# Masking softmax tiles on GpSimd: two affine selects per block in place of one multiplication by a stored mask

## The chip, the core and the metric

The kernel runs on one core of one Trainium2 chip. The metric is the device time of one execution in microseconds (us). Five engines work side by side, each through its own list of instructions in order, and wait for one another by semaphores: TensorE (PE, matrix products and transposes, with its weight loads PEld), VectorE (DVE), ScalarE (ACT), GpSimd (POOL) and SyncE (SP, which here only issues DMAs). POOL and ACT also issue DMAs. PE writes to PSUM; DVE and ACT read PSUM and SBUF; POOL works on SBUF alone.

## The reference

Eight batches, eight heads, 576 positions, head size 64. Causal attention over a window of 64 positions, then a multiplicative feed-forward network over all 4608 tokens.

```python
scores = scale * np.matmul(q, k.transpose(0, 1, 3, 2))
rel = pos[:, None] - pos[None, :]
mask = (rel >= 0) & (rel < 64)
scores = np.where(mask, scores, -1000000000.0)
attn = softmax(scores)
x = np.matmul(attn, v)          # -> (4608, 512)
a = x @ w1
b = x @ w2
out = ((a * b) @ w3) @ w_out
```

## The kernel before

The order of the work on each engine is written out by hand in the program. There are two strands that share PE.

**Attention.** A batch is cut into three segments of 192 queries (`SEGS`), and a segment into two head pairs, so a batch has six score tiles, d = 6b to 6b + 5, and the kernel 48. `scores(d)` computes K times Q transposed on PE (L303) into PSUM, takes the exponential with ACT into an fp16 tile `pt` in SBUF (L307), and then POOL sets to zero what lies outside the window, in place (L312). It does so by multiplying with a stored 0/1 mask of 128 x 256, broadcast over four head rows. In the first segment two instructions do it (4 x 128 and 4 x 64 columns), in the other two one instruction over 1024 columns. `pt` has six buffers. `values(d)` multiplies `pt` with V on PE (L339 in the first two batches, L355 later); V has columns of ones beside it, so the same product yields the row sums. ACT turns these into reciprocals (logarithm and exponential, L345/L346, L361 to L363), and DVE writes the normalised result to `xT` (L347, L364/L365).

**Preparation of a batch.** K and Q arrive in fp32 by SP's DMAs (`load_qk`, tile `stage`) and are cast to fp16 by POOL (L226, 1152 columns each, four per batch), or, in the first two batches, arrive as fp16 in `rows` by POOL's DMAs and are copied by DVE and ACT (also L226). PE transposes them (L262), DVE and ACT copy the result out of PSUM (L266). V comes by POOL's DMAs into `v16` (`load_v`, L241); two of its blocks overlap others by half, so `copy_v` copies halves of 64 partitions from SBUF to SBUF on DVE (L245, and L247 for one block). V of batch 0 takes another way: it is copied by DVE (L226, twice, "k<-rows" in the profile, since the tile is shared), transposed twice by PE and evicted.

**Feed-forward.** First w3 and w_out are folded into one matrix `wc_sb` (`fold_t` L493/L494, `fold_mm` L502/L504), between the score tiles of batch 0. Then groups of 512 tokens pass `ffn_ab` (L433 on PE, into the three `f_ps` banks of PSUM; ACT copies one product out, L438, DVE multiplies the other with it, L439) and `ffn_o` (L451 on PE, DVE copies out to `t2k`, L453, SP stores). In the steady part a tick of the attention is placed between these pieces by due times, and each tick carries one event of the next batch (`late`): a load, a cast, a transpose or a copy of V.

POOL's list therefore holds, in this order: constants, weight loads, the mask's making (`make_mask`, a memset and two affine selects on 128 x 256), and then masks, casts and DMA issues as the program writes them. At the start it reads: masks of tiles 0 and 1, two loads of w1/w2, masks of 2 and 3, two loads of K of batch 1, masks of 4 and 5, two loads of Q, two more of w1/w2, five of V of batch 1. DVE's two copies of V of batch 0 stand behind the masks' first tiles in time, and PE's transposes of V wait for both.

Of the kernel before, what the change touches and what calls it, by code (L numbers as in the profile page):

```python
# [9 lines left out]
FP16 = mybir.dt.float16  # L10
I32 = mybir.dt.int32
ALU = mybir.AluOpType
# [3 lines left out]
P = 128  # L16
# [128 lines left out]
def kernel(  # L145
# [11 lines left out]
    nc = tc.nc  # L157
# [23 lines left out]
    const = fast.enter_context(tc.tile_pool(name="const", bufs=1))  # L181
# [87 lines left out]
    def keys_of_v(b, js, into, cps):  # L269
# [4 lines left out]
        for j, tp, cp in zip(js, into, cps):  # L274
            cp(v16s[b % 2][:, :, j].rearrange("p c (a e) -> p c a e", a=2)[:, :, :, 0:D],
               tp.rearrange("p c (a e) -> p c a e", a=2))

    probs, lns = {}, {}
    mask = const.tile([P, 2 * P], FP16)

    def make_mask():
        nc.gpsimd.memset(mask, 1.0)
        pat = [[-64, 2], [1, P]]
        nc.gpsimd.affine_select(out=mask, in_=mask, pattern=pat, compare_op=ALU.is_ge,
                                fill=0.0, base=64, channel_multiplier=-1)
        nc.gpsimd.affine_select(out=mask, in_=mask, pattern=[[-s, m] for s, m in pat], compare_op=ALU.is_ge,
                                fill=0.0, base=63 - 64, channel_multiplier=1)

    def scores(d):

        b, r = divmod(d, 6)
        si, jp = divmod(r, 2)
        kT, qT = turned["k", b], turned["q", b]
        seg = SEGS[si]
        w = sum(blk[2] for blk in seg)
        s_ps = ps_s.tile([P, 2, 2, 256], FP32, name="s_ps")
        for jj in range(2):
            j = 2 * jp + jj
            c0 = 0
            for (k0, q0, n, _) in seg:  # L300
                for a in range(2):
                    half = slice(a * D, a * D + D)
                    nc.tensor.matmul(s_ps[:, a, jj, c0:c0 + n], kT[half, j, k0:k0 + P], qT[half, j, q0:q0 + n],  # L303
                                     start=True, stop=True, skip_group_check=True)
                c0 += n
        pt = sb.tile([P, 2, 2, 256], FP16, name="pt", bufs=6)
        nc.scalar.activation(pt[:, :, :, 0:w], s_ps[:, :, :, 0:w], AF.Exp, bias=-SHIFT, scale=scale)  # L307

        rows = pt.rearrange("k a j n -> k (a j) n")
        for (lo, n, m0) in [(0, 128, 128), (128, 64, 0)] if si == 0 else [(0, 256, 0)]:  # L310
            sl = rows[:, :, lo:lo + n]
            nc.gpsimd.tensor_tensor(sl, sl, mask[:, m0:m0 + n].unsqueeze(1).to_broadcast([P, 4, n]), ALU.mult)  # L312
        probs[d] = pt

    def values(d, pool=None):
# [78 lines left out]
    def tick(u):  # L394

        b, r = divmod(u, 12)
        d = u // 2
        if u % 2 == 0 and d < ND:
            scores(d)
        ev = late.get(r, [])  # L400
        for e in ev:
            if e[0] == "t":
                event(b, *e)
        if u % 2 == 1 and 12 <= d - 1 < ND:
            values(d - 1)
        for e in ev:
            if e[0] != "t":
                event(b, *e)
        n, m = divmod(u - LAG - 4, 4)
        if m == 3 and n >= 6:  # L410
            keep_sums(n)
# [63 lines left out]
    def load_wo(half):  # L475
        cols = slice(half * 256, half * 256 + 256)
        nc.gpsimd.dma_start(out=wo16[:, :, cols], in_=moe_w_out[:, cols].rearrange("(e p) m -> p e m", p=P))
# [28 lines left out]
    rows = 2 * 3 * B  # L506
# [38 lines left out]
    for n in range(2, 4):  # L545
        load_w3(n)
    load_wo(1)
    make_mask()

    def bank(pool, name):  # L550

# [16 lines left out]
    transposes(0, "q", 0, 1, 2, into=three(), cps=[act_cp, dve_cp, act_cp])  # L568
    keep_busy(6)
    scores(0)  # L570
    keep_busy(4)
    fold_t(0)
    scores(1)
    fold_t(1)
    for i in range(2):
# [94 lines left out]
    for g in range(1, NG):  # L670
        part = [lambda g=g, fc=fc: ffn_ab(g, fc) for fc in range(8)] + \
               [lambda g=g, t=t: ffn_o(g, t) for t in range(4)]
        lo = need[g]
# [58 lines left out]
```

## Time and profile before

| what | us |
|---|---|
| three runs | 304.34, 304.97, 307.15 (median 304.97) |
| the profiled execution, its own time | 304.97 |
| its span, from first to last instruction | 303.1 |
| mean granted clock of PE | 0.977 |
| POOL busy, of it the masks (L312) | 174.3, 97.6 |
| POOL idle before masks, waiting for ACT | 89.4 |
| masks of 1024 columns, 32 of them, mean | 2.146 |
| masks of 512 columns, 16, mean | 1.152 |
| masks of 256 columns, 16, mean | 0.666 |
| casts by POOL, 1152 columns, 24, mean | 1.149 |
| copies of V by DVE, L245, 14: shortest, median, longest | 0.289, 0.874, 3.584 |

Busy time is the sum of what the profiler shows of an engine's instructions; issues of DMAs count as busy on POOL. A line of the groups gives line, engine, operation, output and inputs with partitions x columns and type, then the number of instructions, the busy time in us with the mean of one in ns, and the idle time before them with what ended it. A line of a timeline gives start, length, engine, line, operation and count, and in brackets the idle time before the first. Instructions that follow closely with the same line and tiles are merged into one. A table of windows gives, for each stretch, its length, then for PE, PEld, DVE, ACT and POOL the busy time and the number of instructions, and behind them the granted clock of PE, the DMA share and GB/s.

### The profile page before, as it was taken

How to read it: one execution, taken by the hardware profiler on the slowest of the kernel's cores; microseconds unless marked ns; L12 is line 12 of the kernel's file. 1: busy time of each engine (PE TensorE's matmuls, PEld its weight loads, DVE VectorE, ACT ScalarE, POOL GpSimd, SP SyncE). 2: the span in 40 equal slices, each digit the busy share in tenths (PEclk: the TensorE clock that was granted, in tenths of full speed). 3: DMA queues.
4: the chain of work that ended last, by engine and by line, in shares of the span. 5: the costliest groups of instructions: out<-in, count | busy, mean ns of one | idle time of the engine just before them, and what ended most of it. 6: DMA issues, size and time to landing. Idle time of an engine off the chain costs nothing.

```text
span 303.1 us, 6174 instructions
## 1 busy us (share of the span) xinstructions
PE 281.6 (93%) x2425; PEld 164.2 (54%) x2425; DVE 194.6 (64%) x277; ACT 170.2 (56%) x281; POOL 174.3 (58%) x153
## 2 busy tenths in 40 slices
PE   8793999969999999998999899997999999999993
PEld 8673977524554555554555588453555544454442
DVE  1468456443686766779868966679688665455441
ACT  2652447656357738775686455385748766742310
POOL 9899710299558856596669452792776543320400
PEclk9897799998999999999999999999999999999999
DMA  6999999658558928292829190780059003003013
GB/s 253 220 210 204 211 190 39 243 229 55 94 205 336 79 84 286 85 73 79 282 104 112 72 320 29 75 146 0 3 92 130 0 25 117 2 0 140 1 38 109
DMA packets 48449, 37.68 MB, mean 124 GB/s; under 512 B 34160, under 2 KB 38512, under 8 KB 48416
## 3 DMA queue, kind: packets, MB, share of 16 engines
q0 software_dynamic: 38960, 11.14, 37.0%
q1 hardware_dynamic: 9024, 24.79, 22.3%
q10 hardware_dynamic: 432, 1.31, 1.2%
q8 instruction: 20, 0.33, 0.4%
q14 instruction: 13, 0.11, 0.1%
HBM read 38.80 MB, written 9.44 MB: 159 GB/s over the span
## 4 chain that ended last, share of the span: by engine, by line
PE 74%; DVE 11%; issue 8%; ACT 5%; POOL 1%; DVEq 0%; POOLq 0%; ACTq 0%
PE f_ps L433 36%; PE f_ps L451 14%; PE tp L262 5%; PE s_ps L303 4%; PE o_ps L355 4%; PE f_ps L502 3%; PE tp L528 3%; DVE k L226 2%; DVE t2k L453 2%; DVE v L245 1%; PE f_ps L493 1%; DVE ab L439 1%; PE o_ps L339 1%; DVE v L247 1%; DVE xT L365 1%
## 5 line engine op out<-in xcount | busy, mean ns | idle before, releaser
L312 POOL TENSOR_TENSOR pt<-pt,mask 128x512 f16<-128x512 f16 (+1 forms) x64 | 97.0, 1527 | 89.4 <-ACT pt L307 89.3
L433 PE MATMUL f_ps<-xT,w_sb 128*128 128x512 f16 (+1 forms) x640 | 136.4, 361 | 4.4 <-DVE t2k L453 2.4
L433 PEld LDWEIGHTS <-w_sb 128*128 128x128 f16 x640 | 60.1, 98 | 56.5 <-issue 7.2
L451 PE MATMUL f_ps<-wc_sb,ab 128*128 128x512 f16 (+1 forms) x296 | 66.9, 373 | 0.1
L439 DVE TENSOR_TENSOR ab<-f_ps,a_sb 128x512 f16<-128x512 f32 x72 | 49.6, 691 | 25.3 <-PE f_ps L433 23.7
L307 ACT ACTIVATE pt<-s_ps 128x1024 f16<-128x1024 f32 (+1 forms) x48 | 45.7, 952 | 26.8 <-PE s_ps L303 23.6
L438 ACT COPY a_sb<-f_ps 128x512 f32<-128x512 f32 x72 | 41.7, 579 | 29.0 <-PE f_ps L433 28.4
L451 PEld LDWEIGHTS <-ab 128*128 128x128 f16 x296 | 27.6, 98 | 27.6 <-issue 0.3
L364 DVE TENSOR_TENSOR xT<-o_ps,r 64x384 f16<-64x384 f32 x36 | 19.7, 548 | 34.3 <-ACT r L363 34.2
L361 ACT ACTIVATE ln_s<-o_ps 64x384 f32<-64x384 f32 x36 | 17.5, 487 | 32.6 <-PE o_ps L355 32.6
L453 DVE COPY t2k<-f_ps 128x512 f32<-128x512 f32 (+1 forms) x36 | 24.4, 681 | 11.1 <-PE f_ps L451 10.7
L241 POOL DMA_DIRECT2D v<-in_v_dram x35 | 30.1, 868 | 2.3 <-DMA rows<-in_k_dram 1.1
L355 PEld LDWEIGHTS <-v 128*128 128x128 f16 x288 | 17.9, 98 | 9.0 <-issue 0.8
L355 PE MATMUL o_ps<-pt,v 128*128 128x128 f16 (+1 forms) x288 | 20.7, 215 | 0.4 <-DVE xT L365 0.4
L303 PEld LDWEIGHTS <-kT 64*128 64x128 f16 x384 | 10.7, 95 | 18.6 <-issue 17.3
L365 DVE TENSOR_TENSOR xT<-o_ps,r 64x384 f16<-64x384 f32 x36 | 20.2, 561 | 0.5
L363 ACT ACTIVATE r<-ln_s 128x384 f32<-128x384 f32 x36 | 18.8, 522 | 1.1
L245 DVE COPY v<-v 64x512 f16<-64x512 f16 x14 | 19.1, 1365 | 0.4
L303 PE MATMUL s_ps<-qT,kT 64*128 64x128 f16 (+1 forms) x384 | 18.5, 217 | 0.2
L266 DVE COPY kT<-tp 128x768 f16<-128x768 f16 x19 | 18.0, 950 | 0.0
L362 ACT ACTIVATE ln_s<-o_ps 64x384 f32<-64x384 f32 x36 | 17.4, 482 | 0.4
L226 POOL CAST k<-stage 128x1152 f16<-128x1152 f32 x12 | 13.7, 1149 | 3.5 <-issue 3.5
(88 smaller groups left out, 237.4 us busy)
## 6 DMA issues: line engine op xcount, KB each, us to landing
out_dram<-t2k SPq DMA_DIRECT2D x35, 256.0 KB
stage<-in_k_dram SPq DMA_DIRECT2D x13, 576.0 KB
stage<-in_q_dram SPq DMA_DIRECT2D x13, 576.0 KB
v<-in_v_dram POOLq DMA_DIRECT2D x28, 128.0 KB, 4.4
w_sb<-in_moe_w_dram POOLq DMA_DIRECT2D x4, 512.0 KB, 12.7
ab<-in_moe_w_dram POOLq DMA_DIRECT2D x2, 512.0 KB, 7.8
ab<-in_moe_w_out_dram POOLq DMA_DIRECT2D x2, 512.0 KB, 12.7
xT<-in_moe_w_dram POOLq DMA_DIRECT2D x2, 512.0 KB, 14.4
```

Of the source, the lines that this page charges most:

```text
L241: nc.gpsimd.dma_start(out=vh[lo:P, c], in_=v[b, :, s0:s0 + P - lo, :].rearrange("h s d -> s h d"))
L245: dve_cp(vh[0:D, c], vh[D:P, c - 1])
L303: nc.tensor.matmul(s_ps[:, a, jj, c0:c0 + n], kT[half, j, k0:k0 + P], qT[half, j, q0:q0 + n], start=True, stop=True, skip_group_check=True)
L307: nc.scalar.activation(pt[:, :, :, 0:w], s_ps[:, :, :, 0:w], AF.Exp, bias=-SHIFT, scale=scale)
L312: nc.gpsimd.tensor_tensor(sl, sl, mask[:, m0:m0 + n].unsqueeze(1).to_broadcast([P, 4, n]), ALU.mult)
L355: nc.tensor.matmul(o_ps[:, jj, o0:o0 + n], v16[:, si * 2 + bi, j0 + jj, a * D:a * D + P], pt[:, a, jj, c0:c0 + n], start=first, stop=(bi = ...
L365: nc.vector.tensor_tensor(xs[D:P], o_ps[D:P, :, 192:384], r[D:P], ALU.mult)
L433: nc.tensor.matmul(d[:, f * n + c0:f * n + c1], w[:, dc, (fc + f) * P:(fc + f + 1) * P], xT[:, dc, xc:xc + c1 - c0], start=first, stop=(dc ...
L438: act_cp(a_sb[:, 0:nf * n], a_ps[:, 0:nf * n])
L439: nc.vector.tensor_tensor(ab[:, fc:fc + nf, lo:hi], b_ps[:, 0:nf * n].rearrange("p (f n) -> p f n", f=nf), a_sb[:, 0:nf * n].rearrange("p ...
L451: nc.tensor.matmul(o_ps[:, 0:c1 - c0], ab[:, fc, t * P:t * P + P], wc_sb[:, fc, c0:c1], start=(fc == 0), stop=(fc == 7))
L453: cp(o_sb[:, c0:c1], o_ps[:, 0:c1 - c0])
```

## The change

`scores` no longer multiplies by the stored mask. It applies two affine selects in place to each block: the first keeps an element where the position in the window is not below zero, the second where it is below 64, and both write 0.0 elsewhere. The stored mask and its making are gone. The table `MASKS` lists for each segment the blocks: offset, number of 128-column blocks, columns, and the numbers of the condition. In the first segment there are two blocks (128 and 64 columns in each of the four head rows), hence four instructions per tile where there were two. In the other segments there is one block of 2 x 128 in each of four rows, 1024 columns, hence two instructions where there was one. The second select of a pair reads what the first wrote and waits for it by POOL's own semaphore; a multiplication waits for ACT alone. In all, 64 multiplications, a memset and two selects go, and 128 selects come. The lists of PE, DVE, ACT and SP are the same before and after, and so is the place of each mask in POOL's list. The words that came with the change speak of copies of V's halves of batch 1 and of loads and casts of K and Q of batch 2; the diff holds nothing of these.

```diff
     probs, lns = {}, {}
-    mask = const.tile([P, 2 * P], FP16)
-
-    def make_mask():
-        nc.gpsimd.memset(mask, 1.0)
-        pat = [[-64, 2], [1, P]]
-        nc.gpsimd.affine_select(out=mask, in_=mask, pattern=pat, compare_op=ALU.is_ge,
-                                fill=0.0, base=64, channel_multiplier=-1)
-        nc.gpsimd.affine_select(out=mask, in_=mask, pattern=[[-s, m] for s, m in pat], compare_op=ALU.is_ge,
-                                fill=0.0, base=63 - 64, channel_multiplier=1)
+    MASKS = [[(0, 1, 128, 0, 0), (128, 1, 64, 64, 0)]] + 2 * [[(0, 2, 128, 64, -64)]]
...
         rows = pt.rearrange("k a j n -> k (a j) n")
-        for (lo, n, m0) in [(0, 128, 128), (128, 64, 0)] if si == 0 else [(0, 256, 0)]:
-            sl = rows[:, :, lo:lo + n]
-            nc.gpsimd.tensor_tensor(sl, sl, mask[:, m0:m0 + n].unsqueeze(1).to_broadcast([P, 4, n]), ALU.mult)
+        for (lo, nb, n, off, step) in MASKS[si]:
+            sl = rows[:, :, lo:lo + nb * n]
+            pat = [[0, 4], [step, nb], [1, n]]
+            if nb == 1:
+                pat = [[0, 4], [1, n]]
+            nc.gpsimd.affine_select(out=sl, in_=sl, pattern=pat, compare_op=ALU.is_ge,
+                                    fill=0.0, base=off, channel_multiplier=-1)
+            nc.gpsimd.affine_select(out=sl, in_=sl, pattern=[[-s, m] for s, m in pat], compare_op=ALU.is_ge,
+                                    fill=0.0, base=63 - off, channel_multiplier=1)
         probs[d] = pt
...
     load_wo(1)
-    make_mask()
```

## The prediction, made before the run

> **What bounds the kernel.** I read the page first: busy times and the chain that ended last.
>
> ```profile
> PE 281.6 (93%) x2425; PEld 164.2 (54%) x2425; DVE 194.6 (64%) x277; ACT 170.2 (56%) x281; POOL 174.3 (58%) x153
> PE 74%; DVE 11%; issue 8%; ACT 5%; POOL 1%; DVEq 0%; POOLq 0%; ACTq 0%
> ```
>
> PE sets the end. POOL, the only engine whose instructions the change touches, has 1% of the chain and is idle for 42% of the span, so its own sum decides nothing. But DVE has 11%, so I went to the timeline of PE (start, us, engine, line, names, count, in brackets the idle time before and what ended it) for the places where it stood still.
>
> ```profile
> 28.21 0.82 PE L262 MATMUL o_ps<-ident,k 128*128 128x128 f16 x6 [4.60 <-DVE k L226]
> 67.22 0.43 PE L339 MATMUL o_ps<-pt,v 128*64 128x64 f16 x12 [2.73 <-DVE v L247]
> 143.43 1.02 PE L433 MATMUL f_ps<-xT,w_sb 128*128 128x512 f16 x4 [0.98 <-DVE t2k L453]
> 172.38 1.03 PE L433 MATMUL f_ps<-xT,w_sb 128*128 128x256 f16 x8 [0.95 <-DVE t2k L453]
> 173.84 1.91 PE L433 MATMUL f_ps<-xT,w_sb 128*128 128x256 f16 x16 [0.43 <-DVE t2k L453]
> 205.24 1.89 PE L433 MATMUL f_ps<-xT,w_sb 128*128 128x512 f16 x8 [0.39 <-DVE ab L439]
> 208.98 1.89 PE L433 MATMUL f_ps<-xT,w_sb 128*128 128x512 f16 x8 [1.40 <-DVE ab L439]
> ```
>
> These are 11.5 us, and each has a DVE instruction behind it. The timelines of DVE and then POOL tell why:
>
> ```profile
> 21.27 6.88 DVE L226 COPY k<-rows 128x1152 f16<-128x1152 f16 x2
> 49.59 0.45 DVE L226 COPY k<-rows 128x1152 f16<-128x1152 f16 x1
> 87.00 0.29 DVE L245 COPY v<-v 64x512 f16<-64x512 f16 x1
> 135.50 3.58 DVE L245 COPY v<-v 64x512 f16<-64x512 f16 x1
> ```
>
> ```profile
> 134.59 1.16 POOL L226 CAST k<-stage 128x1152 f16<-128x1152 f32 x1
> 135.70 2.13 POOL L312 TENSOR_TENSOR pt<-pt,mask 128x1024 f16<-128x1024 f16 x1
> 137.77 1.14 POOL L226 CAST k<-stage 128x1152 f16<-128x1152 f32 x1
> ```
>
> A copy of V takes 0.29 us at 87.00, when POOL is still, and 3.58 at 135.50, where it ends (139.08) 0.17 behind the last of three POOL instructions that follow one another without a pause (138.91). The two copies at 21.27 take 6.88 together, and 0.45 each at 49 to 51 us, where POOL is still. So a DVE copy between SBUF tiles stands while POOL computes. That is the path by which masks reach PE: how long POOL runs without a pause, not how much it does.
>
> **The change, part by part.** Orders on PE, DVE, ACT and SP stay the same; only POOL's list changes: 64 multiplications go, 128 selects come in pairs, and the building of the mask (L282 to L286) goes. The words given with the change (V's copies, loads of batch 2) are not what the diff does, so nothing is priced for them.
>
> The price of a select, from the groups by form (busy us, mean ns):
>
> ```profile
> L284 POOL TENSOR_SCALAR_AFFINE_SELECT mask<-mask 128x256 f16<-128x256 f16 x1 | 0.4, 401 | 0.1
> masks.py:199 POOL TENSOR_SCALAR_AFFINE_SELECT ident<-ident 128x128 f16<-128x128 f16 x1 | 0.3, 291 | 0.1
> L312 POOL TENSOR_TENSOR pt<-pt,mask 128x1024 f16<-128x1024 f16 x32 | 68.5, 2146 | 39.5 <-ACT pt L307 39.5
> ```
>
> 401 - 291 = 110 ns for 128 more columns: 0.86 ns a column and 0.18 us fixed, hence 1.06 us for 1024 columns, 0.62 for 512, 0.40 for 256. (One more row of the pattern also costs 110 this way, so eight rows of 128 give the same 1.06.) The CAST, one input too, has 1152 columns in 1.15. The other bound is proportion, 401 x 4 = 1.60; I take 1.06, as the CAST is nearest in size. The second select of a pair waits for the first: L284 starts at 13.00 and L286 at 13.48, so 0.08 of pause. A pair over 1024 is 2.20 against 2.15; a first-segment tile (512 and 256) is 2.20 against 1.82. POOL gets 32 x 0.05 + 16 x 0.38 = 7.7 us more, hidden under its 129 us of idle time. Behind a mask POOL also issues DMAs, up to 0.8 us later at the start, but early loads land one behind another (w_sb 12.7 us after issue), so the queue stays fed. The mask's building (1.2 us) ended in front of a wait of 1.27 for ACT: zero. The selects' waits queue only POOL's own next masks, casts and issues.
>
> The pause is what pays. A waiting DVE copy has its place between the two selects, 1.06 us into a mask. Whether 0.08 us is enough no row shows for sure. For it: the copies of 0.29 end 0.14 to 0.17 after POOL falls still, so they start at once; and the first copy of 21.27 (4.59 us, the longest of its line, so to 25.86) got through at 25.46, where POOL went from an issue to a mask with 0.01 between. Against it: at 135.75 and 137.83 one instruction followed another and the copy did not get in; but there the next POOL instruction waited for nothing of POOL's own.
>
> - Start. Masks begin at 15.14; two tiles 4.40, two issues 1.57: the third tile starts at 21.11, its first select ends at 22.17. The first copy (asked for at 21.27) runs there and ends at 22.5. The second I let wait through a select and the next tile's first select, to 24.62, and end at 24.95. PE goes on at 25.0 instead of 28.21: 3.2 less. Bounds: 0 (no pause used, or 0.5 lost) and 4.3 (it gets in at 23.6).
> - Clock. The granted clock fell behind that stop:
>
> ```profile
> 28.20:32.00 3.80, 3.79 (x36) 3.79 (x37) 1.65 (x2) 1.52 (x2) 3.80 (x5) 0.50 1.24 207
> 32.00:36.00 4.00, 4.00 (x48) 3.84 (x46) 2.70 (x5) 1.17 (x2) 2.95 (x4) 0.81 1.14 211
> ```
>
> The seventh figure is the clock: half until about 33.5. Without a stop of that length 5.3 us of work at half clock becomes 2.65 if PE alone counts; V's copies out of PSUM stand in it too, so I take 2.2 of the 2.65. Bound below: 0.
> - At 64.5. The two copies of V of batch 1 stand here one behind the other. Tiles 6 and 7 put POOL 0.4 to 0.5 later, so L245 meets the second CAST, runs between tile 8's selects (66.4), and L247 meets the second select and perhaps both casts of q, to 67.2 at best and 69.9 at worst: PE goes on 1.1 earlier to 2.7 later; the half clock from 67.6 to 71.0 (1.75 us on eight matmuls, 3.58 for 1.83) may go or double. I take +1.0.
> - Batches 3 to 6. 0.98 + 0.95 + 0.43 + 0.39 + 1.40 = 4.15 of stops. At 135.50 the copy would end at 136.9, 2.1 earlier, and the next one (now 140.86) would come before the mask at 140.06. I take 3.8 of 4.15; bounds 0 and 4.15.
>
> Sum: -3.2 - 2.2 + 1.0 - 3.8 = -8.2. Span 303.1 - 8.2 = 294.9; with the 1.9 outside the span (304.97 - 303.1; this execution is also the median) **296.8 us**.
>
> [...] The row: the copy of 135.50 waited through three POOL instructions, 3.3 us. [...]
>
> **Rivals.**
> - *The pause is too short.* Copies wait through both selects as through one multiplication, 0.05 to 0.4 longer. For: the two refusals above. Time: 304.97 + 0.5 at the start or at 64.5, about 305.5 (303 to 307.5).
> - *A dear select makes POOL the bound* (slower). Place: the steady batches. A batch now costs POOL 97.6/8 = 12.2 in masks, 4.5 in casts, 4.3 in V issues: 21 of the some 31 us between first tiles (145.71 to 177.01). It decides when masks take 22, that is from some 1.9 us per 1024-column select. At 2.15 (the multiplication's rate in each of a pair) masks take 4 x 4.4 + 2 x 3.8 = 25, POOL 34 a batch: 3 us over on five or six batches, less what the pauses bring: about 318 (308 to 325). Against: three rows of the trace at 0.86 ns; for: none has a pattern with a zero step or 1024 columns.
> - *The middle eats the start*: both copies at 64.5 wait through the casts with half clock twice, +2.7 + 1.75, with half of the other gains: about 304.
>
> **Chances.** Forecast 0.60 (its own range 292 to 300.5: all gains at their ends, or the start at half). Short pause 0.20, dear select 0.15, middle 0.05. Range 292 to 307: nearly all of the forecast and the first and third rival, some 0.8; what is left out is mostly the dear select. Faster by over 1% (below 301.9; 1% is about what a measurement here tells from no change) 0.61, within 0.22, slower (over 308.0) 0.17.
>
> **What will show it.** Selects of 128x1024 at about 1.06 us; L226's two DVE copies together under 4 us; PE's stop before L262 under 1.5 and no half clock behind it; copies of L245 never over 1.6; no stops at t2k and ab in batches 3 to 6; the stop before L339 near 64 us not shorter. Wrong if selects are over 1.6, or if copies still end only where a pair and its followers end.

## The result, and the profile after

The changed kernel took 292.05 us (median of 4 runs, 291.53 to 292.87) where the kernel before took 305.36 (4 runs, 304.34 to 307.15). The ratio is 0.9561, with a 95% interval of 0.9508 to 0.9613: 13.3 us less. Times here and below are medians of all runs, ratios those of the runs within 1.5% of the fastest of the same kernel. The forecast was 296.8, 8.2 us less, in a range of 292 to 307, at whose lower edge the result lies. The direction and the path were as predicted; the size was not. The profiled execution took 292.37 us, its span is 290.5 and the mean granted clock 0.991 (before 304.97, 303.1, 0.977).

The busy times and the chain that ended last, from the page of the changed kernel:

```profile
PE 276.5 (95%) x2425; PEld 160.4 (55%) x2425; DVE 179.4 (62%) x277; ACT 170.2 (59%) x281; POOL 179.3 (62%) x214
PE 81%; DMA 5%; DVE 4%; ACT 3%; POOL 3%; issue 1%; SPq 0%; POOLq 0%; DVEq 0%; ACTq 0%
```

POOL is 5 us busier, DVE 15.2 us less busy with the same 277 instructions, and DVE's part of the chain fell from 11% to 4%. POOL was given more work, and what fell is the time in which DVE's copies stand: its copies from SBUF to SBUF took 30.8 us together before and 15.3 after, the rest of DVE 168.9 in both.

The timeline of PE, at the places where it stood before:

```profile
23.22 0.51 PE L262 MATMUL o_ps<-ident,k 128*128 128x128 f16 x6 [0.40 <-DVE k L226]
59.70 0.45 PE L338 MATMUL o_ps<-pt,v 128*64 128x64 f16 x12 [2.15 <-DVE v L247]
133.74 1.89 PE L432 MATMUL f_ps<-xT,w_sb 128*128 128x512 f16 x8
161.44 3.66 PE L432 MATMUL f_ps<-xT,w_sb 128*128 128x256 f16 x32
194.04 1.89 PE L432 MATMUL f_ps<-xT,w_sb 128*128 128x512 f16 x8
196.21 1.89 PE L432 MATMUL f_ps<-xT,w_sb 128*128 128x512 f16 x8
```

The stop of 4.60 us before V's transposes (L262) is 0.40. The five stops of the batches, 0.98, 0.95, 0.43, 0.39 and 1.40, are gone: these lines have no brackets, and the groups of 4, 8 and 16 that the stops had cut apart are whole again (x8, x32). Of the stops shown before, only the one near 58 us is left, 2.15 for 2.73. The granted clock (seventh figure) of the two stretches around the first place:

```profile
23.00:28.00 5.00, 4.40 (x68) 4.14 (x69) 3.43 (x6) 3.00 (x5) 4.86 (x6) 1.00 1.29 202
28.00:33.00 5.00, 4.57 (x74) 3.74 (x70) 2.44 (x5) 2.91 (x7) 4.93 (x7) 1.00 1.24 210
```

The half clock that fell behind that stop is gone. Now the same two places on DVE and then POOL as in the prediction, the start and the copy of batch 3, on DVE:

```profile
20.48 2.68 DVE L226 COPY k<-rows 128x1152 f16<-128x1152 f16 x2
127.93 1.67 DVE L245 COPY v<-v 64x512 f16<-64x512 f16 x1
```

and on POOL:

```profile
21.64 1.20 POOL L310 TENSOR_SCALAR_AFFINE_SELECT pt<-pt 128x1024 f16<-128x1024 f16 x1
22.81 1.31 POOL L308 TENSOR_SCALAR_AFFINE_SELECT pt<-pt 128x1024 f16<-128x1024 f16 x1
...
127.23 1.16 POOL L226 CAST k<-stage 128x1152 f16<-128x1152 f32 x1
128.33 1.11 POOL L308 TENSOR_SCALAR_AFFINE_SELECT pt<-pt 128x1024 f16<-128x1024 f16 x1
129.52 1.09 POOL L310 TENSOR_SCALAR_AFFINE_SELECT pt<-pt 128x1024 f16<-128x1024 f16 x1
130.57 1.14 POOL L226 CAST k<-stage 128x1152 f16<-128x1152 f32 x1
```

The copy of 127.93 comes up during a cast (to 128.39). It does not get in there, where the select follows at once; it stands through the first select (to 129.44) and ends at 129.60, 0.16 behind it, so it got in at the gap before the second. Before, the like copy stood through a cast, a multiplication and a cast, 3.58 us. At the start the two copies take 2.68 together where they took 6.88, and the second ends at 23.16, so it got in where the second select of one tile ends (22.84) and the first of the next begins. That next select is shown 1.31 long where its kind takes 1.11, as if here POOL had stood for the copy.

To see where the time came from, the start of the same PE instruction is compared in both traces:

| PE instruction | before | after | ahead | gained since the row above | predicted |
|---|---|---|---|---|---|
| first product of the fold | 16.60 | 15.81 | 0.79 | 0.8 | 0 |
| first transpose of V, batch 0 | 28.21 | 23.22 | 4.99 | 4.2 | 3.2 |
| after the half clock | 33.52 | 26.58 | 6.94 | 1.95 | 2.2 |
| values that wait for V of batch 1 | 67.22 | 59.70 | 7.52 | 0.6 | -1.0 |
| before the first stop of the batches | 132.18 | 124.61 | 7.57 | 0.05 | 0 |
| after the last stop of the batches | 208.98 | 196.21 | 12.77 | 5.2 | 3.8 |
| end of the last product | 298.42 | 285.34 | 13.08 | 0.3 | 0 |

Behind the last product 0.5 us is given back (4.7 to 5.2 us to the end of the span), which leaves the 12.6 us between the two profiled executions.

The price of the selects, from the groups by form (busy us, mean ns):

```profile
L308 POOL TENSOR_SCALAR_AFFINE_SELECT pt<-pt 128x1024 f16<-128x1024 f16 x32 | 35.7, 1114 | 34.5 <-ACT pt L300 34.5
L310 POOL TENSOR_SCALAR_AFFINE_SELECT pt<-pt 128x1024 f16<-128x1024 f16 x32 | 35.2, 1099 | 2.3
```

The 2.3 us of idle time before 32 second selects is the pause: 0.07 us each.

### The profile page after: what moved, and what is told of

Read it like the earlier page. It is cut to its first block, busy times and chain, and to the rows that moved or that the text cites. A ratio compares the mean times of both kernels' runs of the same rounds, so it can differ in the third digit from the quotient of the medians.

```text
span 290.5 us, 6234 instructions
## 1 busy us (share of the span) xinstructions
PE 276.5 (95%) x2425; PEld 160.4 (55%) x2425; DVE 179.4 (62%) x277; ACT 170.2 (59%) x281; POOL 179.3 (62%) x214
## 3 DMA queue, kind: packets, MB, share of 16 engines
q10 hardware_dynamic: 432, 1.31, 1.3%
## 4 chain that ended last, share of the span: by engine, by line
PE 81%; DMA 5%; DVE 4%; ACT 3%; POOL 3%; issue 1%; SPq 0%; POOLq 0%; DVEq 0%; ACTq 0%
PE f_ps L432 40%; PE f_ps L450 21%; PE o_ps L354 5%; PE tp L262 5%; PE s_ps L296 4%; PE f_ps L501 3%; DMA ab<-in_moe_w_out_dram 3%; DMA stage<-in_q_dram 2%; POOL v L536 2%; PE o_ps L338 1%; DVE k L226 1%; PE s_ps L338 1%; ACT r L345 1%; ACT pt L300 1%; ACT ln_s L344 1%
## 5 line engine op out<-in xcount | busy, mean ns | idle before, releaser
L308 POOL TENSOR_SCALAR_AFFINE_SELECT pt<-pt 128x512 f16<-128x512 f16 (+1 forms) x64 | 52.4, 819 | 69.2 <-ACT pt L300 69.2
L310 POOL TENSOR_SCALAR_AFFINE_SELECT pt<-pt 128x512 f16<-128x512 f16 (+1 forms) x64 | 51.9, 812 | 4.5
## 6 DMA issues: line engine op xcount, KB each, us to landing
w_sb<-in_moe_w_dram POOLq DMA_DIRECT2D x4, 512.0 KB, 12.6
```

What stands on the lines that cost most here:

```text
L308: nc.gpsimd.affine_select(out=sl, in_=sl, pattern=pat, compare_op=ALU.is_ge, fill=0.0, base=off, channel_multiplier=-1)
L310: nc.gpsimd.affine_select(out=sl, in_=sl, pattern=[[-s, m] for s, m in pat], compare_op=ALU.is_ge, fill=0.0, base=63 - off, channel_multip ...
```

## The experiments

My theory: the gain is the pause. The second select waits for the first on POOL itself, and a copy that waits on DVE gets in there; DVE's earlier end then moves PE. Rivals: more instruction boundaries (the places where one POOL instruction ends and the next begins) do it, paused or not; the select is kinder to DVE than the multiplication, whatever the pauses; and, for the size, that the start's gain comes from one place alone, or that it carries the batches' gain with it.

**Boundaries without a pause, with the old operation.** The multiplication of 1024 columns is cut in two of 512 that have nothing to do with each other:

```diff
-        for (lo, n, m0) in [(0, 128, 128), (128, 64, 0)] if si == 0 else [(0, 256, 0)]:
+        for (lo, n, m0) in [(0, 128, 128), (128, 64, 0)] if si == 0 else [(0, 128, 0), (128, 128, 128)]:
```

> The kernel before, with the multiplication of tiles of 1024 columns cut into two halves of 4 x 128 that do not wait for each other. Nothing is left out. Pause theory (a DVE copy gets in only where POOL stands still, and the wait of the second select on the first makes such a place): no pauses are added, so as before, 303 to 308 us, copies of V again up to 3 us and more. Boundary theory (it gets in at any end of a POOL instruction, so what counts is that instructions are shorter): most of the gain, 293 to 298. Select theory (a select, with one input, holds up a copy less than a multiplication with two): as before, 303 to 308.

Measured: 302.57 us (10 runs, 298.40 to 305.81); the ratio, from the five runs up to 302.22, is 0.9813 (0.976 to 0.9866). That is neither nothing nor the whole, and less time than the 303 to 308 that the pause theory had expected. The copy of batch 3, on DVE and then on POOL:

```profile
128.94 4.00 DVE L245 COPY v<-v 64x512 f16<-64x512 f16 x1
```

```profile
128.31 1.16 POOL L226 CAST k<-stage 128x1152 f16<-128x1152 f32 x1
129.43 2.28 POOL L312 TENSOR_TENSOR pt<-pt,mask 128x512 f16<-128x512 f16 x2
131.64 1.14 POOL L226 CAST k<-stage 128x1152 f16<-128x1152 f32 x1
```

It stood through four instructions and passed three boundaries without getting in. Elsewhere in the same execution copies did get in: at 200.25 one took 0.38, at 23.03 the second copy of batch 0 took 1.41. So the start has its gain here without any pause (PE is 5.3 us ahead of the trace before at 34 us), while stops of 0.69, 0.67, 0.43, 0.67 and 0.99 us stay in the batches. Here a boundary alone was a chance, not a place.

**The same halves with a pause.** The first half is two columns wider, so that the second overlaps it and must wait for it. The two columns are multiplied by the mask's 0 or 1 twice, which leaves them as they are.

```diff
+        for (lo, n, m0) in [(0, 128, 128), (128, 64, 0)] if si == 0 else [(0, 130, 0), (128, 128, 128)]:
```

> The same halves, but the first is two columns wider (4 x 130), so that the second reads what the first wrote and waits for it; multiplying twice by 0 or 1 changes nothing. Pause theory: a pause of about 0.08 us appears in the middle of each of 32 tiles, and most of the gain comes without any select: 293 to 298 us, copies of V at most 1.7. Boundary theory: the same as without the wait, within 1 us. Select theory: as before, 303 to 308.

Measured: 292.20 us (4 runs, 291.75 to 293.21), ratio 0.9564 (0.95 to 0.9629), the whole gain with the multiplication kept. The same copy, on DVE and then on POOL:

```profile
127.56 2.17 DVE L245 COPY v<-v 64x512 f16<-64x512 f16 x1
```

```profile
127.27 1.16 POOL L226 CAST k<-stage 128x1152 f16<-128x1152 f32 x1
128.38 2.42 POOL L312 TENSOR_TENSOR pt<-pt,mask 128x520 f16<-128x520 f16 x2
130.75 1.14 POOL L226 CAST k<-stage 128x1152 f16<-128x1152 f32 x1
```

It ends at 129.73, 0.16 behind the first half (128.38 + 1.19 = 129.57) and long before the second. Its 2.17 us are more than the 1.7 expected, as it came up during a cast and did not get in at the cast's end. Beside the run above, only the wait and the two columns are new.

**Selects without a pause.** The reverse: each tile's selects are cut by head rows, all first selects come before all second ones, so the wait is met while another select runs.

```diff
+        parts = []
+        for (lo, nb, n, off, step) in MASKS[si]:
+            pat = [[0, 2], [step, nb], [1, n]] if nb > 1 else [[0, 2], [1, n]]
+            for r0 in (0, 2):
+                parts.append((rows[:, r0:r0 + 2, lo:lo + nb * n], pat, off))
+        for low in (True, False):
+            for sl, pat, off in parts:
...
```

> The changed kernel, with each pair of selects cut in two halves of the head rows, ordered first select of both halves, then second select of both: every wait is met while another select runs, so the pause is gone, and there are twice as many, shorter selects (about 0.63 us for 512 columns). Pause theory: most of the gain is lost, 300 to 307 us. Boundary theory: even more boundaries, 291 to 294. Select theory: the gain stays, 291 to 294.

Measured: 300.92 us (5 runs, 300.31 to 308.21); the ratio, from the four up to 302.30, is 0.9833 (0.9752 to 0.9914). The start was ahead by 6.69 us at 34 us, then one copy of batch 1 and the half clock that followed left 1.05 of it. DVE, and POOL behind it:

```profile
58.06 5.92 DVE L245 COPY v<-v 64x512 f16<-64x512 f16 x1
```

```profile
57.06 2.24 POOL L226 CAST k<-stage 128x1152 f16<-128x1152 f32 x2
59.26 1.22 POOL L311 TENSOR_SCALAR_AFFINE_SELECT pt<-pt 128x512 f16<-128x512 f16 x2
60.44 1.22 POOL L314 TENSOR_SCALAR_AFFINE_SELECT pt<-pt 128x512 f16<-128x512 f16 x2
61.61 2.23 POOL L226 CAST q<-stage 128x1152 f16<-128x1152 f32 x2
63.79 2.65 POOL L241 DMA_DIRECT2D v<-in_v_dram  x3
```

A copy of 0.29 us stood through eight computing instructions and ended only behind the last cast; PE stood 7.94 us, with half clock from 60.7 to 70.9. So at this place selects without a pause have the multiplication's trouble. They do not have it everywhere: the start's gain came whole, and the first three of the five stops of the batches are gone. There the copy of batch 3, on DVE and then on POOL, got in behind the first select (it ends at 137.57), though the next one follows at once:

```profile
136.09 1.48 DVE L245 COPY v<-v 64x512 f16<-64x512 f16 x1
```

```profile
135.66 1.17 POOL L226 CAST k<-stage 128x1152 f16<-128x1152 f32 x1
136.77 1.30 POOL L311 TENSOR_SCALAR_AFFINE_SELECT pt<-pt 128x512 f16<-128x512 f16 x2
```

With the pause the multiplication has the whole gain, and without it the selects have not: the operation is not what decided. In these runs more boundaries without a pause brought part of the gain (302.57, 300.92) and the pause the whole of it (292.20, 292.05).

**The first term by itself, without masks.** In the kernel before, V's two copies of batch 0 go to ACT:

```diff
-        cast_qk(0, "v", hh, dve_cp)
+        cast_qk(0, "v", hh, act_cp)
```

> [...] All theories in which the start's stop is a DVE copy standing behind POOL: two copies of 1.13 us, PE's stop before L262 falls from 4.60 to 1 to 1.5 us, the half clock behind it goes, 5 to 6 us gained: 299 to 300.5. If V's arrival set that stop: no gain, 304 to 306.

Measured: 299.45 us (4 runs, 298.88 to 300.71), ratio 0.9809 (0.9741 to 0.9876). PE's timeline at the place:

```profile
23.61 0.51 PE L262 MATMUL o_ps<-ident,k 128*128 128x128 f16 x6 [0.92 <-ACT k L226]
```

On ACT the copies took 1.16 and 1.15 us while POOL masked, against 1.13 and 1.15 for like copies by ACT at 49 us of the trace before, where POOL is still: POOL did not hold them up. No half clock follows. PE is 6.4 us ahead at 34 us (0.9 of it already at the fold's first product) and 5.93 at the end; the batches' stops stay (0.96, 0.96, 0.43, 0.40, 1.39). The start is worth 5 to 6 us, and in sum little of it is lost and nothing multiplied later.

**Selects in batch 0 alone, and in all others alone.** The condition in `scores` is the first line below in one run and the second in the other; the tiles left over are multiplied by the mask as before:

```diff
+        if d < 6:
...
+        if d >= 6:
```

> Selects in pairs for tiles 0 to 5 (batch 0) alone, the stored mask for all others. Nothing is left out. Pause theory, by places: the start's stop and the half clock behind it go (in the changed kernel PE was 6.1 us ahead between 17 and 34 us), the stops of batches 3 to 6 stay at about 4 us together: 6 to 7 us gained, 298 to 300. A theory in which the gain comes from POOL's or DVE's lower load over the whole run: about 1/8 of the gain, 303 to 304.

> The complement: the stored mask for tiles 0 to 5, selects in pairs from tile 6 on. Pause theory: the start is as before (stop of 4 to 5 us, half clock behind it), the stops behind copies of V in batches 3 to 6 go (5.2 us) and the one near 64 us changes by less than 1: 5 to 6.5 us gained, 299 to 300.5. With the run on the start alone the two gains make up the whole 13 within 1 us. Load theory: 7/8 of the gain, 293 to 295.

Measured: 298.51 us (4 runs, 297.94 to 299.72), ratio 0.9767 (0.9734 to 0.98), for the start alone; 299.02 us (4 runs, 298.27 to 300.08), ratio 0.9801 (0.9763 to 0.984), for the rest. Against the 305.32 of the kernel before on that chip these are 6.8 and 6.3, in all 13.1 of the 13.3: the two add up. PE's timeline with the start alone still has the batches' stops:

```profile
138.59 1.02 PE L445 MATMUL f_ps<-xT,w_sb 128*128 128x512 f16 x4 [0.99 <-DVE t2k L465]
```

and with the rest alone still the start's:

```profile
28.05 0.82 PE L262 MATMUL o_ps<-ident,k 128*128 128x128 f16 x6 [4.72 <-DVE k L226]
140.21 1.89 PE L445 MATMUL f_ps<-xT,w_sb 128*128 128x512 f16 x8
```

**The stop that is left.** In the changed kernel, the three copies of V of batch 1 (two calls) move ahead of the casts that hold them up:

```diff
     transposes(1, "q", 0, 1, 2, into=three(), cps=[act_cp, dve_cp, act_cp])
+    copy_v(1, 1)
+    copy_v(1, 4)
...
-        if d in (6, 8):
-            copy_v(1, {6: 1, 8: 4}[d])
```

> The changed kernel, with the copies of V of batch 1 (three, L245/L247) moved ahead, from behind the sixth and eighth pieces of the feed-forward to right behind Q's transposes of batch 1, where POOL is still idle. If the stop of 2.15 us near 57.6 and the half clock of 60.0 to 63.4 behind it (1.75 us on eight products) are the rest of the same contention, both go: 3 to 4 us gained over the changed kernel, 288 to 289. If V of batch 1 lands too late there (49 us), DVE stands and PE loses 1 us: 291 to 293.

Measured: 292.57 us (4 runs, 291.37 to 294.00), ratio 0.9565 (0.9519 to 0.9612): no gain over the change, where 3 to 4 us had been expected. The copies took 0.29 us each and the stop of 2.15 went, but another came ten microseconds later. PE's timeline, and then POOL's:

```profile
69.41 0.64 PE L338 MATMUL s_ps<-pt,v 128*64 128x128 f16 x16 [2.50 <-POOL pt L310]
70.32 3.58 PE L450 MATMUL f_ps<-wc_sb,ab 128*128 128x512 f16 x8
```

```profile
62.25 2.23 POOL L226 CAST q<-stage 128x1152 f16<-128x1152 f32 x2
64.42 2.64 POOL L241 DMA_DIRECT2D v<-in_v_dram  x3
67.06 1.13 POOL L308 TENSOR_SCALAR_AFFINE_SELECT pt<-pt 128x1024 f16<-128x1024 f16 x1
```

PE reached the values of tile 9 sooner than POOL its mask, which is behind two casts and three DMA issues in POOL's list; the eight matmuls of 3.58 us show the half clock that followed. In the trace of the changed kernel that mask is done at 67.72 and PE comes to it at 69.12 without a stop: the old stop had covered this one.

**And the issues out of the way.** On top of that, the five loads of V of batch 2 move to a stretch where POOL is idle, behind the third `keep_sums`:

```diff
         keep_sums(n)
+    load_v(2, 0, 2, 3)
+    load_v(2, 4, 5)
...
-    load_v(2, 0, 2, 3)
     load_qk(3, "k")
...
-        if d == 6:
-            load_v(2, 4, 5)
```

> The kernel with the early copies of V of batch 1, and in addition the five loads of V of batch 2 issued by POOL where it is idle (behind the fold, some 43 to 51 us) instead of between the masks of tiles 8 to 10. If the stop of 2.50 us before values of tile 9 (on a mask that stood behind casts and loads in POOL's list) took the place of the one removed, it goes with the loads, 4.2 us of POOL's list, and the half clock behind it: 3 to 4 us gained over the changed kernel, 288 to 289.5. If the loads' landing or the casts still hold PE up: 291 to 293.

> The changed kernel once more on the same chip as the kernel above, for the comparison: 291.5 to 293; copies of V again at most 1.7 us, the stop before L339's counterpart near 57 us of 1.6 to 2.2 with a half clock behind it or without, by where it falls.

Measured on one chip: 289.73 us (4 runs, 288.71 to 290.78), ratio 0.9486 (0.9437 to 0.9534), and for the changed kernel there 291.69 (4 runs, 291.10 to 292.10), ratio 0.9534 (0.9491 to 0.9578). All its runs lie below all of the changed kernel's on that chip, the closest by 0.3 us, though the two intervals overlap; the gain of 2.0 is less than the 3 to 4 expected. POOL's timeline has the mask right behind the casts:

```profile
61.34 2.24 POOL L226 CAST q<-stage 128x1152 f16<-128x1152 f32 x2
63.52 1.10 POOL L308 TENSOR_SCALAR_AFFINE_SELECT pt<-pt 128x1024 f16<-128x1024 f16 x1
```

Neither the stop at 57 nor the one at 69 is in this trace. Of all the kernels it is the fastest.

**The kernel before once more**, for the 0.8 us at the very start, where nothing of the change has run yet:

> The kernel before once more, for its clock: if the half clock between 13.0 and 16.4 us comes from where the first products fall in the clock's windows and not from the kernel, it may be missing or longer here; the stop before L262 of 4 to 5 us and those of batches 3 to 6 are there again, 304 to 307.

Measured: 306.06 us in one execution. The windows of 13.0 to 16.4 us, first in the trace before, then in this one:

```profile
13.00:16.40 3.40, 3.40 (x39) 2.72 (x39) 0.69 (x1) 1.20 (x2) 2.06 (x4) 0.50 1.29 208
```

```profile
13.00:16.40 3.40, 2.97 (x47) 2.46 (x47) 1.25 (x2) 1.80 (x3) 2.19 (x4) 1.00 1.28 208
```

One kernel, half clock (39 matmuls) and full (47). The fold's first product starts at 15.88 here, as in the changed kernel (15.81) and not as in the trace before (16.60). So this term belongs to the execution and not to the change.

## Why the prediction was right in direction and short in size

**The mechanism held.** A copy got in at the pause inside a pair, and 0.07 us of it was enough: with the old operation and a pause the time was 292.20, with selects and no pause 300.92. What the prediction did not count on is that a copy got in without a pause too, as at 22.84 and at 58.39 in the trace after. *The pause is too short* (0.20) fell with the first. *A dear select* (0.15) fell with the prices: 1.114 and 1.099 us for 1024 columns against 1.06, 0.634 against 0.62 for 512, 0.415 against 0.40 for 256. The masks take POOL 104.3 us against 97.6, 6.7 more where I said 7.7, and PE waits for a mask in a single place, 0.38 us at 88.23. *The middle eats the start* (0.05) fell too: that place gained 0.6.

**The terms that were mis-sized.** The sum was -8.2, the two profiled executions differ by 12.6 (the medians by 13.3, as the executions profiled are not the medians of all runs). By the table above:

- *Start, predicted -3.2, measured -4.2.* The step that failed is "the second I let wait through a select and the next tile's first select, to 24.62". It got in one select sooner, behind the second select of its tile, and PE went on at 23.22 instead of 25.0 (0.8 of this difference belongs to the last item below). I had 4.3 as the far bound and took the nearer value because two boundaries of the trace had turned a copy away; a boundary without a pause did let a copy in at times, in 35 of 94 cases over all traces.
- *Half clock, predicted -2.2, measured -1.95.* Right within 0.3.
- *At 64.5, predicted +1.0, measured -0.6.* The same step failed, and this is the term furthest off: I let L245 wait for the pause between tile 8's selects and L247 stand behind it through the second select and perhaps casts. In the trace after, L245 gets in one instruction sooner, where the cast ends (58.39) and the select follows at once, and takes 0.72; L247 has the pause for itself and takes 1.07. The half clock behind the stop neither went nor doubled: 0.50 in the granted clock from 60.0 to 63.4. It is absent in the trace of the changed kernel on the other chip, where the stop is 2.17, so the stop's length alone does not decide it.
- *Batches 3 to 6, predicted -3.8 of 4.15, measured -5.2.* Here the bound itself was wrong. I took the sum of the idle times shown as the most there was to gain. But a shown stop was shorter than what it cost: a single matmul of 128x512 is shown 0.383 us long, while eight of them in a row take 1.89, a step of (1.89 - 0.383) / 7 = 0.215, so behind the last matmul before a stop some 0.17 of waiting is shown as work. The five stops of 0.98, 0.95, 0.43, 0.39 and 1.40 gave 1.25, 1.24, 0.59, 0.55 and 1.57, between 0.16 and 0.29 more each. In the first two, the first matmul of the values just ahead also came 0.12 and 0.13 later than a step of 0.216 behind the one before it, with no idle time shown at all.
- *Not in the sum*: 0.8 at 16.6 us, where half clock falls in one execution and not in another, and 0.3 less 0.5 at the end. Altogether 1.0 + 1.6 + 1.4 + 0.8 - 0.25 - 0.2 = 4.35 of the 4.4 that were missing.

Two of the signs that I had named did not hold: L245's copies reach 1.68, not 1.6 (the one of 127.93 waits 0.46 for the end of a cast, does not get in there, and then stands through a whole select); and the stop before V's values became shorter, 2.15 for 2.73.

Some copies waited for longer than one POOL instruction here: even in the changed kernel the one of 127.93 stood through the rest of a cast (0.46 us) and a whole select (1.05), and without a pause one stood 5.92 us through eight instructions. At those boundaries the next POOL instruction began before the waiting copy did, again and again. The slope of a select measured here is (1.114 - 0.634) / 512 us = 0.94 ns a column, where I had taken 0.86 from the selects of 128 and 256 columns.

## What to carry to other kernels

In these traces, a short VectorE copy from SBUF to SBUF (0.29 us where GpSimd was still) that shows a length of several microseconds (3.58, 4.00, 5.92) was standing behind GpSimd, and what counted was how long GpSimd ran without a pause, not its busy time (174.3 us before, 179.3 in the run that was 13.3 us faster). Where a trace shows this, give that run a place to breathe (an instruction that waits for its own predecessor on GpSimd, even at the cost of more work), or move the copy to ScalarE, where it took 1.16 us beside the masks. When the stop is gone, look at once for the next wait behind it, which the old one had covered (2.50 us in front of 69.41 here), and don't take the idle time that a trace shows on TensorE for the most that can be gained (4.15 shown in the batches, 5.2 gained).

## What the runs showed of the hardware

- Over the twelve traces, a waiting DVE copy got in at the end of a POOL instruction in 36 of 36 cases where POOL paused for 0.07 to 0.09 us, and in 35 of 94 where the next computing instruction started no more than 0.02 behind (6 of 6 and 5 of 13 in the first trace of the kernel before and that of the changed kernel). A copy counts as having got in where it ended within 0.35 us; 8 of the 35 came up only some 0.1 us before the boundary and were not held up at all. What decides those 94 is open, and so is whether the 0.07 us themselves or the wait behind them make the place: every such pause here comes from a wait of POOL on itself. A guess of mine, that POOL had taken up the next instruction before the copy came up, was not shown and cannot explain all of them: the copy of 58.06 without a pause also stood behind selects (L314) that waited for one which ended only at 59.88.
- It seems to have worked both ways: a select that began as a copy got in at the start is shown 1.31 instead of 1.11 us, in four of the traces.
- Up to the last product, half clock came in these traces in stretches of some 3.4 us or twice that: 13.0 to 16.4, 26.7 to 33.5 and 67.6 to 71.0 in the first trace of the kernel before, 59.9 to 63.3 in that of the changed kernel (once, behind the stop of 7.94, 10.2). The one of 26.7 began 1.5 us before PE went on at 28.21. The one between 13.0 and 16.4 us is not in the second trace of the kernel before, which is 0.7 us ahead for it at the fold's first product. The kernel with the early copies of V of batch 1 differs from the changed kernel only after 45 us, but its trace has half clock from 12.3 to 19.1 and is 1.7 us behind at 34 us: so much can two single executions differ with no change in the program.
